# Retention and a gated convolution on one core: from one head's 128-row tile at a time to chunks of all heads with a running state, x kept on chip, and the convolution on TensorE

## The chip, the core and the metric

The kernel runs on one core of a Trainium2 chip. Its time is what the device measures from start to end, in microseconds. Each kernel is timed several times; of the kernel before three runs are given: 1052.33 us in the median, 1052.18 to 1053.14. The profile is of one execution, and its span (first to last instruction) was 1050.2 us.

## The reference

Inputs are q, k and v, each (batch 8, heads 8, positions 576, 64 columns) in float32, two weight matrices 512 x 512 and five rows of convolution weights 5 x 512.

```
scores = q @ k.T / 8                              # per batch and head
ret    = scores * gamma[h] ** (i - j) for i >= j, 0 otherwise
attn   = ret @ v                                  # gamma[h] = 1 - 2 ** (-5 - h)
x      = heads side by side: (batch, 576, 512)
gate   = sigmoid(sum over kk of conv_w[kk] * x shifted down by 4 - kk positions)
out    = (gate * (x @ w_val)) @ w_out             # (8, 576, 512) float32
```

## The kernel before

The work stands in two stages, and the order inside each is the order in which the program's loops write it.

The first stage loops over 8 batches and 8 heads. For one head it takes the 576 positions as four tiles of 128 and one of 64. Each tile of k and q is loaded (L86, 128 rows of 64 floats, one DMA on SyncE's queue, three buffers for all of them), cast to bfloat16 on GpSimd (L87), transposed on TensorE (L88) and copied from PSUM by ScalarE (L89). v is loaded and cast (L94, L95). Then, for each query tile, a loop over the key tiles up to it makes the scores (L103, contraction over 64 rows), multiplies them by a decay table on VectorE (L106 on the diagonal, L109 under it) and adds their product with v into one PSUM tile (L112). A head has 15 such blocks, the program 960. The result is cast on ScalarE (L115) and written to a tensor `xT` in device memory (L116), transposed: columns of the model by positions, in bfloat16.

The second stage loops over batches and, in each, over the position tiles. It loads a batch's `xT` (L146) with four zero columns in front. For each of four blocks of 128 columns it makes x @ w_val in four matmuls of 128 columns (L153), makes the convolution on VectorE in one multiplication (L157) and four multiply-adds (L159) over shifted slices, applies the sigmoid on ScalarE (L163) and multiplies gate and value on VectorE (L164). Four matmuls of 512 columns (L167) make the output tile, ScalarE copies it (L170) and SyncE's queue writes it out (L171). All DMAs of both stages are issued by SyncE.

The lines that the change replaces most are these of the innermost loops:

```
sc_ps = ps.tile([sk, sq], F32)
nc.tensor.matmul(sc_ps, lhsT=kall[:, j0:j0 + sk], rhs=qall[:, i0:i0 + sq], start=True, stop=True)
nc.vector.scalar_tensor_tensor(g, in0=xT_sb[:, dop, c0 + kk:c0 + kk + sz],
                               scalar=cw_sb[:, kk, dop:dop + 1], in1=g, op0=ALU.mult, op1=ALU.add)
```

Of the kernel before, what the change touches and what calls it, by code (L numbers as in the profile page):

```python
# [17 lines left out]


@with_exitstack  # L20
def kernel(
# [20 lines left out]
    dec_pool = ctx.enter_context(tc.tile_pool(name="dec", bufs=16))
    sb = ctx.enter_context(tc.tile_pool(name="sb", bufs=3))
    actx = ExitStack()
    vpool = actx.enter_context(tc.tile_pool(name="vp", bufs=2))
    ps = actx.enter_context(tc.tile_pool(name="ps", bufs=2, space=bass.MemoryType.PSUM))
    ops = actx.enter_context(tc.tile_pool(name="ops", bufs=2, space=bass.MemoryType.PSUM))

    q_tiles = [(i, min(128, S - i)) for i in range(0, S, 128)]
    j_tiles = q_tiles  # L50

    dec_full = {}
    dec_diag = {}
    gammas = {}
    for h in range(H):
        gamma = 1.0 - 2.0 ** (-5.0 - h)
        gammas[h] = gamma
        lng = math.log(gamma)
        it = sb.tile([128, 128], mybir.dt.int32)
        nc.gpsimd.iota(it, pattern=[[1, 128]], base=0, channel_multiplier=-1)  # L60
        ftf = sb.tile([128, 128], F32)
        nc.scalar.activation(ftf, it, AF.Exp, scale=lng)
        ftfull = dec_pool.tile([128, 128], BF16, tag=f"df{h}", bufs=1)
        nc.gpsimd.tensor_copy(ftfull, ftf)
        ftd = dec_pool.tile([128, 128], BF16, tag=f"dd{h}", bufs=1)
        nc.scalar.activation(ftd, ftf, AF.Copy, scale=scale)
        nc.gpsimd.affine_select(ftd, ftd, pattern=[[1, 128]], base=0,
                                channel_multiplier=-1, compare_op=ALU.is_ge, fill=0.0)
        dec_full[h] = ftfull
        dec_diag[h] = ftd  # L70

    from concourse.masks import make_identity
    ident = consts.tile([128, 128], BF16)
    make_identity(nc, ident)
    tps = actx.enter_context(tc.tile_pool(name="tps", bufs=2, space=bass.MemoryType.PSUM))

    for b in range(B):
        for h in range(H):
            kall = sb.tile([D, S], BF16)
            qall = sb.tile([D, S], BF16)  # L80
            for (j0, sk) in j_tiles:
                for src, dst in ((k, kall), (q, qall)):
                    tmpf = sb.tile([128, D], F32, tag="ttmpf")
                    tmp = sb.tile([128, D], BF16, tag="ttmp")
                    tp = tps.tile([D, 128], BF16)
                    nc.sync.dma_start(out=tmpf[:sk], in_=src[b, h, j0:j0 + sk, :])  # L86
                    nc.gpsimd.tensor_copy(tmp[:sk], tmpf[:sk])  # L87
                    nc.tensor.transpose(tp, tmp, ident)  # L88
                    nc.scalar.copy(dst[:, j0:j0 + sk], tp[:, :sk])  # L89
            v_tiles = {}  # L90
            for (j0, sk) in j_tiles:
                v_sbf = vpool.tile([sk, D], F32, tag=f"vsbf{j0}")
                v_sb = vpool.tile([sk, D], BF16, tag=f"vsb{j0}")
                nc.sync.dma_start(out=v_sbf, in_=v[b, h, j0:j0 + sk, :])  # L94
                nc.gpsimd.tensor_copy(v_sb, v_sbf)  # L95
                v_tiles[j0] = v_sb
# [105 lines left out]
```

## Time and profile before

| what | value |
| --- | --- |
| timed runs, median of 3 | 1052.33 us (1052.18 to 1053.14) |
| span of the profiled execution | 1050.2 us, 15367 instructions |
| TensorE matmuls (PE) | 680.8 us busy, 65%, 3360 of them |
| TensorE weight loads (PEld) | 349.4 us, 33% |
| VectorE (DVE) | 463.3 us, 44% |
| ScalarE (ACT) | 296.3 us, 28% |
| GpSimd (POOL) | 233.3 us, 22% |
| DMA | 164813 packets, 50.35 MB, of which 154992 packets under 512 B |

The profiled execution is the one that all rows come from; its span is its own time, and the timed runs stand 2.1 us above it. A busy share is an average over the whole span, so it is read stage by stage. The first stage ends at about 808 us. A matmul's busy time holds its way through the array, so that matmuls that follow each other overlap in it; how fast the array takes them is read from when they start.

### The profile page before, as it was taken

The page shows a single profiled execution, that of the slowest core. Times are in us where ns is not written, and L with a number is a line of the kernel's source. Part 1 is how long each engine was busy: PE and PEld are TensorE (multiplying, and loading weights), DVE is VectorE, ACT ScalarE, POOL GpSimd, SP SyncE. Part 2 cuts the span into 40 slices and gives each one's busy share as a digit, 9 for nine tenths or more (in the row PEclk, how much of TensorE's full clock was granted, in tenths as well). Part 3 has the DMA queues.
Part 4 walks back from the last instruction along what each step waited for, and adds up shares of the span by engine and source line. Part 5 has one row for each costly group of instructions (what it writes and reads, how often), then busy time and mean ns, then how long its engine had stood idle before and what let it go on. Part 6 is the DMA issues. An engine that isn't in the chain of part 4 may idle for free.

```text
span 1050.2 us, 15367 instructions
## 1 busy us (share of the span) xinstructions
PE 680.8 (65%) x3360; PEld 349.4 (33%) x3360; DVE 463.3 (44%) x1928; ACT 296.3 (28%) x1178; POOL 233.3 (22%) x992
## 2 busy tenths in 40 slices
PE   3676666666666666666666666666664567666665
PEld 1333333333333333333333333333332333333332
DVE  1332322222223322223322222222232999999998
ACT  3322222222222222222222222222222233232322
POOL 5222222222222222222222222222222000000000
PEclk9999999999999999999999999999999999998555
DMA  2111111121111111122111111112213121111211
GB/s 78 40 40 44 42 42 41 43 45 42 43 41 42 43 42 41 42 44 44 43 41 42 41 42 41 43 40 45 44 43 90 50 69 58 69 62 64 69 35 46
DMA packets 164813, 50.35 MB, mean 48 GB/s; under 512 B 154992, under 2 KB 159088, under 8 KB 164720
## 3 DMA queue, kind: packets, MB, share of 16 engines
q1 hardware_dynamic: 164720, 49.38, 19.3%
q14 instruction: 67, 0.55, 0.2%
q8 instruction: 26, 0.43, 0.2%
HBM read 35.14 MB, written 14.16 MB: 47 GB/s over the span
## 4 chain that ended last, share of the span: by engine, by line
PE 29%; DMA 28%; DVE 20%; issue 8%; ACT 8%; SPq 4%; POOL 3%; POOLq 1%; ACTq 0%; DVEq 0%
DMA tmpf<-in_q_dram 12%; DVE g L159 12%; PE o_ps L112 10%; PE sc_ps L103 10%; DMA tmpf<-in_k_dram 10%; PE tp L88 7%; DMA v_sbf<-in_v_dram 5%; ACT qall L89 5%; DVE zT L164 3%; POOL tmp L87 3%; DVE g L157 2%; ACT o_sb L115 2%; SPq L116 1%; PE op L167 1%; SPq L86 1%
## 5 line engine op out<-in xcount | busy, mean ns | idle before, releaser
L109 DVE SCALAR_TENSOR_TENSOR d_sb<-sc_ps,ftfull 128x128 bf16<-128x128 f32 (+1 forms) x640 | 151.4, 261 | 431.3 <-PE sc_ps L103 422.9
L112 PE MATMUL o_ps<-d_sb,v_sb 128*64 128x128 bf16 (+2 forms) x960 | 256.6, 268 | 52.5 <-DVE d_sb L109 18.5
L103 PE MATMUL sc_ps<-qall,kall 64*128 64x128 bf16 (+2 forms) x960 | 205.3, 266 | 114.8 <-ACT qall L89 114.1
L88 PE MATMUL tp<-ident,tmp 128*64 128x128 bf16 x640 | 187.3, 313 | 114.8 <-POOL tmp L87 101.5
L87 POOL CAST tmp<-tmpf 128x64 bf16<-128x64 f32 (+1 forms) x640 | 149.7, 236 | 494.3 <-DMA tmpf<-in_k_dram 217.9
L103 PEld LDWEIGHTS <-kall 64*128 64x128 bf16 (+1 forms) x960 | 97.8, 102 | 244.1 <-issue 191.1
L159 DVE SCALAR_TENSOR_TENSOR g<-xT_sb,cw_sb,g 128x128 f32<-128x128 bf16 (+1 forms) x640 | 175.8, 331 | 0.3
L88 PEld LDWEIGHTS <-tmp 128*64 128x64 bf16 x640 | 79.1, 132 | 218.1 <-POOL tmp L87 159.3
L106 DVE TENSOR_TENSOR d_sb<-sc_ps,ftd 128x128 bf16<-128x128 f32 (+1 forms) x320 | 87.8, 274 | 141.2 <-PE sc_ps L103 140.4
L112 PEld LDWEIGHTS <-v_sb 128*64 128x64 bf16 (+1 forms) x960 | 117.4, 136 | 72.0 <-POOL v_sb L95 10.1
L115 ACT CAST o_sb<-o_ps 64x128 bf16<-64x128 f32 (+1 forms) x320 | 79.4, 248 | 199.5 <-issue 120.8
L89 ACT COPY qall<-tp 64x128 bf16<-64x128 bf16 (+1 forms) x320 | 79.4, 248 | 199.3 <-PE tp L88 191.1
L89 ACT COPY kall<-tp 64x128 bf16<-64x128 bf16 (+1 forms) x320 | 79.6, 249 | 175.4 <-PE tp L88 173.5
L167 PE MATMUL op<-w_out_sb,zT 128*128 128x512 bf16 (+1 forms) x160 | 97.8, 620 | 35.4 <-DVE zT L164 35.3
L153 PE MATMUL vp<-xT_sb,w_val_sb 128*128 128x128 bf16 (+1 forms) x640 | 88.7, 293 | 48.1 <-DVE zT L164 40.1
L153 PEld LDWEIGHTS <-w_val_sb 128*128 128x128 bf16 x640 | 66.8, 137 | 95.2 <-issue 94.6
L95 POOL CAST v_sb<-v_sbf 128x64 bf16<-128x64 f32 (+1 forms) x320 | 75.4, 236 | 76.2 <-DMA v_sbf<-in_v_dram 67.1
L163 ACT ACTIVATE g<-g 128x128 f32<-128x128 f32 (+1 forms) x160 | 47.7, 299 | 134.8 <-DVE g L159 132.0
L157 DVE TENSOR_SCALAR g<-xT_sb,cw_sb 128x128 f32<-128x128 bf16 (+1 forms) x160 | 43.4, 272 | 7.8 <-DMA xT_sb<-xT 7.8
L164 DVE TENSOR_TENSOR zT<-g,vp 128x128 bf16<-128x128 f32 (+1 forms) x160 | 43.4, 272 | 1.4 <-ACT g L163 0.4
L167 PEld LDWEIGHTS <-zT 128*128 128x128 bf16 (+1 forms) x160 | 20.2, 127 | 67.1 <-DVE zT L164 65.6
L170 ACT COPY o_sb<-op 128x512 f32<-128x512 f32 (+1 forms) x40 | 23.4, 585 | 33.7 <-PE op L167 33.4
(16 smaller groups left out, 18.2 us busy)
## 6 DMA issues: line engine op xcount, KB each, us to landing
tmpf<-in_k_dram SPq DMA_DIRECT2D x256, 32.0 KB, 1.8
tmpf<-in_q_dram SPq DMA_DIRECT2D x256, 32.0 KB, 1.8
v_sbf<-in_v_dram SPq DMA_DIRECT2D x256, 32.0 KB, 1.8
out_dram<-o_sb SPq DMA_DIRECT2D x32, 256.0 KB, 2.0
xT_sb<-xT SPq DMA_DIRECT2D x8, 576.0 KB, 3.9
xT<-o_sb SPq DMA_DIRECT2D x256, 16.0 KB, 1.8
v_sbf<-in_v_dram SPq DMA_DIRECT2D x64, 16.0 KB, 1.9
w_val_f<-in_moe_w_val_dram SPq DMA_DIRECT2D x1, 1024.0 KB, 5.6
```

The source lines that it names most:

```text
L87: nc.gpsimd.tensor_copy(tmp[:sk], tmpf[:sk])
L88: nc.tensor.transpose(tp, tmp, ident)
L89: nc.scalar.copy(dst[:, j0:j0 + sk], tp[:, :sk])
L95: nc.gpsimd.tensor_copy(v_sb, v_sbf)
L103: nc.tensor.matmul(sc_ps, lhsT=kall[:, j0:j0 + sk], rhs=qall[:, i0:i0 + sq], start=True, stop=True)
L106: nc.vector.tensor_tensor(d_sb, sc_ps, dec_diag[h][:sk, :sq], op=ALU.mult)
L109: nc.vector.scalar_tensor_tensor(d_sb, in0=sc_ps, scalar=c, in1=dec_full[h][:sk, :sq], op0=ALU.mult, op1=ALU.mult)
L112: nc.tensor.matmul(o_ps, lhsT=v_sb, rhs=d_sb, start=(ji == 0), stop=(ji == len(jts) - 1))
L115: nc.scalar.copy(o_sb, o_ps)
L153: nc.tensor.matmul(vp, lhsT=w_val_sb[:, do, dop * P:(dop + 1) * P], rhs=xT_sb[:, do, pad + c0:pad + c0 + sz], start=(do == 0), stop=(do == ...
L159: nc.vector.scalar_tensor_tensor(g, in0=xT_sb[:, dop, c0 + kk:c0 + kk + sz], scalar=cw_sb[:, kk, dop:dop + 1], in1=g, op0=ALU.mult, op1=AL ...
L167: nc.tensor.matmul(op, lhsT=zT[:, dp, :sz], rhs=w_out_sb[:, dp, :], start=(dp == 0), stop=(dp == DOUT - 1))
```

## The change

The program is written anew, with the order of all instructions as the program states it.

- All eight heads are handled at once. A chunk is 128 positions of one batch (32 such chunks), or the last 64 positions of two batches (four tail chunks): 36 chunks. A chunk's k, q and v come in one DMA each into a 128 x 512 tile (two for a tail), 256 bytes to a packet since one head's row has 64 floats. Loads are issued six chunks ahead, weights on ScalarE's queue.
- The decay is split into a factor per key position, multiplied into v on GpSimd (`cast`), and one per query position, multiplied into the result on VectorE (`take_x`). The scores are only masked.
- Scores are made within a chunk alone. What earlier chunks give comes from a running sum of k times v per head (`update`, `take_state`, `carried`), kept in PSUM and copied to a block-diagonal bfloat16 tile.
- The result x stays in on-chip memory, bfloat16, columns by positions, four batches to a tile; nothing is written to device memory between the stages.
- The convolution is made on TensorE: per tap a 64 x 64 diagonal matrix, 40 matmuls of 256 columns for each unit. A unit is two chunks of the second stage.
- The loop runs over slots. In slot t come the loads of chunk t + 6, casts of t + 4, scores of t + 1, values of t, the state of t, transposes of t + 2; an even slot also has the convolution, gate and value product of unit t // 2 - 1, an odd one its output product.

The core of the diff (the tables of decay factors, masks, diagonals and weights are built once ahead of the loop and left out here):

```diff
--- before.py
+++ after.py
...
-    xT = dram.tile([B, DM, S], BF16)
...
-    for b in range(B):
-        for h in range(H):
...
+    half = ctx.enter_context(tc.tile_pool(name="half", bufs=2))
+    bfp = ctx.enter_context(tc.tile_pool(name="bfp", bufs=4))
+    tp_sb = ctx.enter_context(tc.tile_pool(name="tsb", bufs=3))
+    pp = ctx.enter_context(tc.tile_pool(name="pp", bufs=2))
+    gp = ctx.enter_context(tc.tile_pool(name="gp", bufs=2))
+    op_sb = ctx.enter_context(tc.tile_pool(name="osb", bufs=3))
+    xp = ctx.enter_context(tc.tile_pool(name="xp", bufs=1))
+    ps_t = ctx.enter_context(tc.tile_pool(name="pst", bufs=1, space=PSUM))
+    ps_s = ctx.enter_context(tc.tile_pool(name="pss", bufs=1, space=PSUM))
+    ps_o = ctx.enter_context(tc.tile_pool(name="pso", bufs=1, space=PSUM))
+    ps_st = ctx.enter_context(tc.tile_pool(name="psst", bufs=1, space=PSUM))
+    ps_g = ctx.enter_context(tc.tile_pool(name="psg", bufs=3, space=PSUM))
+    chunks = []
+    for g in range(B // GB):
+        for b in range(g * GB, (g + 1) * GB):
+            chunks += [("full", b, c) for c in range(NCH)]
+        chunks += [("tail", b, NCH) for b in range(g * GB, (g + 1) * GB, 2)]
+    NT = len(chunks)
...
+        def load_chunk(b, c):
+            for name, src in (("k", k), ("q", q), ("v", v)):
+                t = half.tile([P, H, D], F32, name=f"f{name}c", bufs=LA + 1)
+                nc.sync.dma_start(out=t, in_=src[b, :, c * P:(c + 1) * P, :].rearrange("h p d -> p h d"))
+                loaded[name, "full", b, c] = t
+        def load_tail(b):
+            for name, src in (("k", k), ("q", q), ("v", v)):
+                t = half.tile([P, H, D], F32, name=f"f{name}c", bufs=LA + 1)
+                for i in range(2):
+                    nc.sync.dma_start(out=t[i * TAIL:(i + 1) * TAIL],
+                                      in_=src[b + i, :, NCH * P:S, :].rearrange("h p d -> p h d"))
+                loaded[name, "tail", b, NCH] = t
...
+        load(0)
+        load(1)
+        cwn = consts.tile([KC * NP, P], F32, name="cwn")
+        nc.scalar.dma_start(out=cwn, in_=moe_conv_w.rearrange("k (o i) -> (k o) i", i=P))
+        wvf = consts.tile([P, NP, DM], F32, name="wvf")
+        wof = consts.tile([P, NP, DM], F32, name="wof")
+        nc.scalar.dma_start(out=wvf, in_=moe_w_val.rearrange("(o i) n -> i o n", i=P))
+        load(2)
+        wo_src = moe_w_out.rearrange("(pr ab hl p) n -> ab hl p pr n", pr=2, ab=2, hl=2)
+        for (p0, blk, ab, hl) in ((0, 0, 0, 0), (64, 0, 1, 0), (0, 2, 1, 1), (64, 2, 0, 1)):
+            nc.scalar.dma_start(out=wof[p0:p0 + 64, blk:blk + 2, :], in_=wo_src[ab, hl])
+        for t in range(3, LA - 2):
+            load(t)
...
+        def cast(t):
+            kind, b, c = chunks[t]
+            kb = bfp.tile([P, H, D], BF16, name="kb")
+            qb = bfp.tile([P, H, D], BF16, name="qb")
+            vb = bfp.tile([P, H, D], BF16, name="vb")
+            nc.gpsimd.tensor_copy(kb, loaded["k", kind, b, c])
+            nc.gpsimd.tensor_copy(qb, loaded["q", kind, b, c])
+            nc.gpsimd.tensor_tensor(vb, loaded["v", kind, b, c],
+                                    gin[:, c, :].unsqueeze(2).to_broadcast([P, H, D]), op=ALU.mult)
+            bf[t] = (kb, qb, vb)
+        tsb = {}
+        def turn(t):
+            kb, qb, vb = bf[t]
+            ps = ps_t.tile([P, 2, NP, P], BF16, name="tps")
+            for i, src in enumerate((kb, qb)):
+                flat = src.rearrange("p h d -> p (h d)")
+                for pr in range(NP):
+                    nc.tensor.transpose(ps[:, i, pr, :], flat[:, pr * P:(pr + 1) * P], ident)
+            kt = tp_sb.tile([P, NP, P], BF16, name="kt")
+            qt = tp_sb.tile([P, NP, P], BF16, name="qt")
+            nc.vector.tensor_copy(kt, ps[:, 0])
+            nc.scalar.copy(qt, ps[:, 1])
+            tsb[t] = (kt, qt)
+        def scores(t):
+            kt, qt = tsb[t]
+            s = [ps_s.tile([P, NP, P], F32, name=f"s{i}") for i in range(2)]
+            for pr in range(NP):
+                for i in range(2):
+                    r = slice(i * 64, i * 64 + 64)
+                    nc.tensor.matmul(s[i][:, pr, :], lhsT=kt[r, pr, :], rhs=qt[r, pr, :],
+                                     start=(pr == 0), stop=(pr == NP - 1), skip_group_check=True)
+            sps[t] = s
+        def masks(t, i):
+            m = mask if chunks[t][0] == "full" else mask_t
+            p = pp.tile([P, NP, P], BF16, name=f"p{i}")
+            nc.vector.tensor_tensor(p, sps[t][i], m.unsqueeze(1).to_broadcast([P, NP, P]), op=ALU.mult)
+            pt[t, i] = p
+        def carried(t):
+            kind, b, c = chunks[t]
+            o = ps_o.tile([P, NP, P], F32, name="o")
+            ops[t] = o
+            qt = tsb[t][1]
+            if kind == "full":
+                if c:
+                    for pr in range(NP):
+                        nc.tensor.matmul(o[:, pr, :], lhsT=state[b][:, pr, :], rhs=qt[:, pr, :],
+                                         start=(pr == 0), stop=False, skip_group_check=True)
+            else:
+                for pr in range(NP):
+                    for i in range(2):
+                        cs = slice(i * TAIL, (i + 1) * TAIL)
+                        nc.tensor.matmul(o[:, pr, cs], lhsT=state[b + i][:, pr, :], rhs=qt[:, pr, cs],
+                                         start=(pr == 0 and i == 0), stop=False, skip_group_check=True)
+        def values(t):
+            kind, b, c = chunks[t]
+            vb = bf[t][2]
+            o = ops[t]
+            fresh = kind == "full" and c == 0
+            for pr in range(NP):
+                for i in range(2):
+                    r = slice(i * 64, i * 64 + 64)
+                    nc.tensor.matmul(o[r, pr, :], lhsT=vb[:, 2 * pr + i, :], rhs=pt[t, i][:, pr, :],
+                                     start=(fresh and pr == 0), stop=(pr == NP - 1), skip_group_check=True)
+        def take_x(t):
+            kind, b, c = chunks[t]
+            x = xg[b // GB]
+            bl = b % GB
+            if kind == "full":
+                i0 = c * P
+                nc.vector.tensor_tensor(x[:, bl, :, PAD + i0:PAD + i0 + P], ops[t], gout[:, :, i0:i0 + P], op=ALU.mult)
+            else:
+                i0 = NCH * P
+                for i in range(2):
+                    nc.vector.tensor_tensor(x[:, bl + i, :, PAD + i0:PAD + S],
+                                            ops[t][:, :, i * TAIL:(i + 1) * TAIL], gout[:, :, i0:S], op=ALU.mult)
+        def update(t):
+            kind, b, c = chunks[t]
+            if kind != "full":
+                return
+            kb, qb, vb = bf[t]
+            if c == 0:
+                st[b] = ps_st.tile([P, NP, P], F32, name="st")
+            kf, vf = (s.rearrange("p h d -> p (h d)") for s in (kb, vb))
+            for pr in range(NP):
+                cs = slice(pr * P, (pr + 1) * P)
+                nc.tensor.matmul(st[b][:, pr, :], lhsT=kf[:, cs], rhs=vf[:, cs],
+                                 start=(c == 0 and pr == 0), stop=(c == NCH - 1 and pr == NP - 1),
+                                 skip_group_check=True)
+        def take_state(t):
+            kind, b, c = chunks[t]
+            if kind != "full":
+                return
+            s = sbl[b % GB] if c == NCH - 1 else sbd[c % 2]
+            for i in range(2):
+                r = slice(i * 64, i * 64 + 64)
+                nc.scalar.copy(s[r, :, i * 64:i * 64 + 64], st[b][r, :, i * 64:i * 64 + 64])
+            state[b] = s
+        def xs(n, rows, blk, shift):
+            kind, b, c = chunks[2 * n]
+            x = xg[b // GB]
+            if kind == "full":
+                c0 = c * P + shift
+                return x[rows, b % GB, blk, c0:c0 + 2 * P]
+            c0 = NCH * P + shift
+            return x[rows, :, blk, c0:c0 + TAIL]
+        def conv(n):
+            g = [ps_g.tile([P, 2, 2 * P], F32, name="g") for _ in range(2)]
+            lo, hi = slice(0, 64), slice(64, 128)
+            for pr in range(2):
+                a, b = 2 * pr, 2 * pr + 1
+                for kk in range(KC):
+                    for (rows, blk, cols, bank) in ((lo, a, lo, 0), (hi, b, lo, 1), (lo, b, hi, 0), (hi, a, hi, 1)):
+                        nc.tensor.matmul(g[bank][cols, pr, :], lhsT=dg[rows, blk, kk, :], rhs=xs(n, rows, blk, kk),
+                                         start=(pr == 0 and kk == 0), stop=(pr == 1 and kk == KC - 1),
+                                         skip_group_check=True)
+            gps[n] = g
+            gsb[n] = []
+        def gate(n, i):
+            t = gp.tile([P, 2, 2 * P], F32, name=f"gate{i}")
+            nc.scalar.activation(t, gps[n][i], AF.Sigmoid)
+            gsb[n].append(t)
+        def value(n, i):
+            vps = ps_g.tile([P, 2, 2 * P], F32, name="g")
+            for j in range(2):
+                for o in range(NP):
+                    nc.tensor.matmul(vps[:, j, :], lhsT=wvb[:, o, 2 * i + j, :], rhs=xs(n, slice(0, P), o, PAD),
+                                     start=(j == 0 and o == 0), stop=(j == 1 and o == NP - 1), skip_group_check=True)
+            z = gp.tile([P, 2, 2 * P], BF16, name=f"z{i}")
+            nc.vector.tensor_tensor(z, gsb[n][i], vps, op=ALU.mult)
+            zsb[n, i] = z
+        def project(n, i):
+            kind, b, c = chunks[2 * n]
+            o = ps_g.tile([P, DM], F32, name="g")
+            for j in range(NP):
+                nc.tensor.matmul(o, lhsT=zsb[n, j // 2][:, j % 2, i * P:(i + 1) * P], rhs=wob[:, j, :],
+                                 start=(j == 0), stop=(j == NP - 1))
+            ob = op_sb.tile([P, DM], F32, name="ob")
+            nc.scalar.copy(ob, o)
+            if kind == "full":
+                c0 = (c + i) * P
+                nc.sync.dma_start(out=out[b, c0:c0 + P, :], in_=ob)
+            else:
+                for j in range(2):
+                    nc.sync.dma_start(out=out[b + 2 * i + j, NCH * P:S, :], in_=ob[j * TAIL:(j + 1) * TAIL])
+        ok = lambda t: 0 <= t < NT
+        cast(0)
+        cast(1)
+        for slot in range(-2, NT + 2):
+            t = slot
+            n = t // 2 - 1
+            unit = 0 <= n < NT // 2
+            odd = t % 2 == 1
+            if t >= 0 and ok(t + LA - 2):
+                load(t + LA - 2)
+            if ok(t + 4):
+                cast(t + 4)
+            if ok(t + 1):
+                scores(t + 1)
+                masks(t + 1, 0)
+            if ok(t):
+                values(t)
+                take_x(t)
+            if ok(t + 1):
+                masks(t + 1, 1)
+            if unit and not odd:
+                conv(n)
+            if ok(t):
+                update(t)
+                take_state(t)
+            if ok(t + 2):
+                turn(t + 2)
+            if t == -2:
+                prep_conv()
+            if t == -1:
+                prep_wv()
+            if t == 0:
+                prep_wo()
+            if unit and not odd:
+                gate(n, 0)
+                gate(n, 1)
+                value(n, 0)
+                value(n, 1)
+            if unit and odd:
+                project(n, 0)
+                project(n, 1)
+            if ok(t + 1):
+                carried(t + 1)
```

## Rows read from the trace of the kernel before

**Rows 1.** The page's 40 equal slices, busy tenths of two engines.

```profile
PE   3676666666666666666666666666664567666665
...
DVE  1332322222223322223322222222232999999998
```

**Rows 2.** The chain that ended last: shares of the span, by engine and line.

```profile
PE 29%; DMA 28%; DVE 20%; issue 8%; ACT 8%; SPq 4%; POOL 3%; POOLq 1%; ACTq 0%; DVEq 0%
DMA tmpf<-in_q_dram 12%; DVE g L159 12%; PE o_ps L112 10%; PE sc_ps L103 10%; DMA tmpf<-in_k_dram 10%; PE tp L88 7%; DMA v_sbf<-in_v_dram 5%; ACT qall L89 5%; DVE zT L164 3%; POOL tmp L87 3%; DVE g L157 2%; ACT o_sb L115 2%; SPq L116 1%; PE op L167 1%; SPq L86 1%
```

**Rows 3.** Windows: PE, PEld, DVE, ACT, POOL busy (count); clock, DMA share, GB/s.

```profile
20.00:780.00 760.00, 502.81 (x2456) 260.71 (x2455) 224.41 (x922) 210.16 (x919) 212.53 (x913) 1.00 0.19 42
...
890.00:960.00 70.00, 48.56 (x246) 23.55 (x246) 69.51 (x299) 21.23 (x61) 0.00 (x0) 1.00 0.17 59
960.50:963.80 3.30, 1.34 (x12) 0.60 (x10) 3.30 (x15) 0.88 (x3) 0.00 (x0) 1.00 0.60 195
964.00:1050.00 86.00, 56.19 (x282) 27.28 (x282) 80.80 (x342) 25.65 (x73) 0.00 (x0) 0.50 0.14 49
```

**Rows 4.** Costliest groups: line, operation, count, busy, mean ns, idle before.

```profile
L159 DVE SCALAR_TENSOR_TENSOR g<-xT_sb,cw_sb,g 128x128 f32<-128x128 bf16 (+1 forms) x640 | 175.8, 331 | 0.3
...
L157 DVE TENSOR_SCALAR g<-xT_sb,cw_sb 128x128 f32<-128x128 bf16 (+1 forms) x160 | 43.4, 272 | 7.8 <-DMA xT_sb<-xT 7.8
```

**Rows 5.** PE timeline: start us, merged time us, line, tiles, count.

```profile
958.88 0.61 PE L153 MATMUL vp<-xT_sb,w_val_sb 128*128 128x128 bf16 x4
...
961.54 0.38 PE L153 MATMUL vp<-xT_sb,w_val_sb 128*128 128x128 bf16 x4 [0.90 <-DVE zT L164]
961.76 0.38 PE L167 MATMUL op<-w_out_sb,zT 128*128 128x512 bf16 x1
...
964.97 0.63 PE L153 MATMUL vp<-xT_sb,w_val_sb 128*128 128x128 bf16 x4
```

**Rows 6.** DMA issues: tile, queue, count, KB each, median us to landing.

```profile
tmpf<-in_k_dram SPq DMA_DIRECT2D x256, 32.0 KB, 1.8
...
out_dram<-o_sb SPq DMA_DIRECT2D x32, 256.0 KB, 2.0
xT_sb<-xT SPq DMA_DIRECT2D x8, 576.0 KB, 3.9
...
out_dram<-o_sb SPq DMA_DIRECT2D x8, 128.0 KB, 2.4
```

**Rows 7.** Groups by shape: busy us, mean ns, idle before.

```profile
L87 POOL CAST tmp<-tmpf 128x64 bf16<-128x64 f32 x512 | 120.6, 237 | 430.3 <-DMA tmpf<-in_k_dram 207.1 <-DMA tmpf<-in_q_dram 132.7 <-PE sc_ps L103 51.3
...
L153 PE MATMUL vp<-xT_sb,w_val_sb 128*128 128x128 bf16 x512 | 76.2, 306 | 42.0 <-DVE zT L164 34.0 <-DMA xT_sb<-xT 8.0
...
L115 ACT CAST o_sb<-o_ps 64x128 bf16<-64x128 f32 x256 | 66.3, 259 | 72.4 <-PE o_ps L112 66.3 <-PE tp L88 0.7
...
L163 ACT ACTIVATE g<-g 128x128 f32<-128x128 f32 x128 | 39.5, 309 | 117.5 <-DVE g L159 114.8
L164 DVE TENSOR_TENSOR zT<-g,vp 128x128 bf16<-128x128 f32 x128 | 36.5, 286 | 0.2 <-PE vp L153 0.2
...
L170 ACT COPY o_sb<-op 128x512 f32<-128x512 f32 x32 | 18.8, 586 | 26.7 <-PE op L167 26.6
...
L115 ACT CAST o_sb<-o_ps 64x64 bf16<-64x64 f32 x64 | 13.2, 206 | 127.1 <-issue 120.8 <-PE o_ps L112 6.3
...
L163 ACT ACTIVATE g<-g 128x64 f32<-128x64 f32 x32 | 8.2, 257 | 17.3 <-DVE g L159 17.3
...
L164 DVE TENSOR_TENSOR zT<-g,vp 128x64 bf16<-128x64 f32 x32 | 7.0, 218 | 1.2 <-ACT g L163 0.4
...
L125 POOL CAST w_val_sb<-w_val_f 128x2048 bf16<-128x2048 f32 x1 | 1.9, 1887 | 0.0
```

**Rows 8.** SP's DMA issues at the start: start us, time us.

```profile
0.80 0.39 SPq L86 DMA_DIRECT2D tmpf<-in_k_dram  x1
1.24 0.41 SPq L86 DMA_DIRECT2D tmpf<-in_q_dram  x1
```

More of the change, by code (lines that the diff above doesn't have):

```diff
@@ L17 @@
 ALU = mybir.AluOpType
+PSUM = bass.MemoryType.PSUM
 @with_exitstack
@@ L34 @@
     DM = moe_w_val.shape[0]
-    assert D == 64 and DM == H * D
+    KC = moe_conv_w.shape[0]
+    P = 128
+    NP = H // 2
+    NCH = S // P
+    TAIL = S - NCH * P
+    PAD = KC - 1
+    GB = 4
+    LA = 8
+    assert D == 64 and DM == H * D and TAIL == 64 and B % GB == 0 and NP == 4
     scale = 1.0 / math.sqrt(D)
-    dram = ctx.enter_context(tc.tile_pool(name="dram", bufs=1, space=bass.MemoryType.DRAM))
-    xT = dram.tile([B, DM, S], BF16)
+    lng = [math.log(1.0 - 2.0 ** (-5.0 - h)) for h in range(H)]
@@ L41 @@
     consts = ctx.enter_context(tc.tile_pool(name="c", bufs=1))
[L42 to L54, printed above, removed]
-    for h in range(H):
[L56 to L75, printed above, removed]
-    for b in range(B):
-        for h in range(H):
[L79 to L96, printed above, removed]
-            for (i0, sq) in q_tiles:
-                o_ps = ops.tile([D, sq], F32)
-                jts = [jt for jt in j_tiles if jt[0] <= i0]
-                for ji, (j0, sk) in enumerate(jts):
-                    v_sb = v_tiles[j0]
-                    sc_ps = ps.tile([sk, sq], F32)
-                    nc.tensor.matmul(sc_ps, lhsT=kall[:, j0:j0 + sk], rhs=qall[:, i0:i0 + sq], start=True, stop=True)
-                    d_sb = sb.tile([sk, sq], BF16)
-                    if j0 == i0:
-                        nc.vector.tensor_tensor(d_sb, sc_ps, dec_diag[h][:sk, :sq], op=ALU.mult)
-                    else:
-                        c = scale * (gammas[h] ** (i0 - j0))
-                        nc.vector.scalar_tensor_tensor(d_sb, in0=sc_ps, scalar=c,
-                                                       in1=dec_full[h][:sk, :sq],
-                                                       op0=ALU.mult, op1=ALU.mult)
-                    nc.tensor.matmul(o_ps, lhsT=v_sb, rhs=d_sb,
-                                     start=(ji == 0), stop=(ji == len(jts) - 1))
-                o_sb = sb.tile([D, sq], BF16)
-                nc.scalar.copy(o_sb, o_ps)
-                nc.sync.dma_start(out=xT[b, h * D:(h + 1) * D, i0:i0 + sq], in_=o_sb)
@@ L130 @@
-    cw_sb = consts.tile([P, Kc, DOUT], F32)
-    with nc.allow_non_contiguous_dma(reason="conv"):
-        for kk in range(Kc):
-            nc.sync.dma_start(out=cw_sb[:, kk, :], in_=moe_conv_w[kk].rearrange("(do di) -> di do", di=P))
-    xp = ctx.enter_context(tc.tile_pool(name="xp", bufs=2))
-    zp = ctx.enter_context(tc.tile_pool(name="zp", bufs=2))
-    vps = ctx.enter_context(tc.tile_pool(name="vps", bufs=2, space=bass.MemoryType.PSUM))
-    opo = ctx.enter_context(tc.tile_pool(name="opo", bufs=2, space=bass.MemoryType.PSUM))
```

119 lines of the change are left out of this document (75 added, 44 removed).

## The prediction

> **What bounds the kernel now.** I read the page's slices first, then the chain that ended last, then each stage by its windows. The slices [rows 1] show two stages. In the first 31 slices PE stands at 6 or 7 tenths and DVE at 2 or 3; behind them DVE is at 9. The chain [rows 2] says what the first stage lacks: its largest pieces are landings of single loads (k 10%, q 12%, v 5%), then PE, ACT and POOL steps of one head that follow each other. That is latency, one 128-row tile of one head at a time, for 64 heads. The second stage is DVE: in 890 to 960 us it is busy 69.5 of 70 us [rows 3], nearly all of it the five tap products (640 of 331 ns and 160 of 272 ns, 219 us together [rows 4]).
>
> Two more things are to be seen, because they set the floor of the changed kernel.
> TensorE's clock. The windows grant 1.00 before 960.5 us and 0.50 after 964 [rows 3]. But four 128-column matmuls take 0.61 us before 960.5, 0.63 after 964, and 0.38 only in between [rows 5]. So the 1.00 ahead of 960.5 doesn't describe the array: by its own spacing it runs at the level of 1.2 GHz there too, and at 2.4 GHz in those 3.3 us alone. At the upper level the next group starts 0.22 us after four such matmuls (961.54 to 961.76): 55 ns for 128 columns with their weight load hidden. At the lower level it is (0.63 less 0.31 for one of them [rows 7]) / 3 = 107 ns.
> The DMA engines. In 20 to 780 us, where nearly every packet has 256 B, they moved 42 GB/s at a share of 0.19 [rows 3], so 42 / 0.19 = 221 GB/s if they were never idle. In 890 to 960 (1152 and 2048 B) it is 59 / 0.17 = 347 GB/s.
>
> **The change, part by part.** All of it goes together: heads side by side in one 128 x 512 tile, 36 chunks of 128 tokens instead of 960 score blocks, the lower blocks replaced by a running 64 x 64 state, taps on TensorE, x kept in SBUF. The old 1050.2 us fall away whole, so the new time is a sum of its own: start, 17 pairs of slots, end. A pair of slots handles two chunks and one unit (two chunks' worth) of the second stage.
>
> DMA per pair. The loads are 28.3 MB, again as 256 B runs (one head's 64 floats), 110,592 of them as before, but 1024 in an instruction instead of 128. 28.3 / 221 = 128 us, 3.56 us a chunk. The output is 9.44 MB in 2048 B rows: 27 us, 1.51 a unit. The weights are 2.1 MB: 6 us. The xT round trip (4.7 MB each way) is gone. A pair costs 2 x 3.56 + 1.51 = 8.6 us. No row shows a 1024-packet load. Bounds: a 512-packet load of 576 KB lands in 3.9 us [rows 6], 131 packets per us counting its latency, which would make 110592 / 131 = 844 us; below, the 347 GB/s of long packets would make 28.3 / 0.347 = 82 us. I take 128 us, since that is the busy time of this very packet size.
>
> TensorE per pair, in steps of 128 columns: transposes 16, scores 16, carried state 8, values 16, state update 8, taps 40 x 2 = 80, value projection 16 x 2 = 32, output projection 8 x 4 = 32; together 208. At 55 ns that is 11.4 us if each matmul has the array to itself. Scores come in pairs on the two row halves, values on the two column halves, taps on all four quarters. If those run side by side, 8 + 8 + 60 steps fall away: 132 x 55 = 7.3 us. Every K = 64 matmul of before uses the same row half, so no row decides it. I take 7.3, because the operands share neither rows, columns nor bank, and keep 11.4.
> On this the Trainium skill speaks both ways (TensorEngine Tiling, Key Properties): tiles "operate independently", but changing the tiling mode drains the engine; Restrictions and Gotchas adds that column tiling disables fast weight load. By the first rule a pair is 7.3, by its absence 11.4, and the drains come on top; no run here shows it.
> Between shapes of different row and column counts I add 0.1 us per change, about one cold 128-column step, seven times a pair: 0.7 us (from 0 to 1.4).
>
> DVE per pair: 4 masks, 2 kt copies, 2 x products, 2 gate products, all of 512 columns. From 286 ns at 128 and 218 at 64 columns [rows 7], 1.06 ns a column: 693 ns, so 6.9 us. ACT: qt 2 and output 2 of 586 ns (a row), two sigmoids of 309 + 384 x 0.81 = 620, four state copies of 259 + 128 x 0.83 = 365: 5.1 us. POOL: a cast of 512 by 237 at 64 and 1887 at 2048 columns is 610 ns, four of them; the v product with two inputs isn't shown, between 0.6 (a cast) and 1.2 (two passes); I take 1.2: 4.8 us. These three lie beside PE and DMA.
>
> Waits that the order adds. In an even slot PE meets value(n,1), whose PSUM bank is the first tap bank, free only after gate(n,0). ACT reaches that after the state copies (from 1.85 us of the slot on, 0.73), qt (0.59) and the gate (0.62): 3.8 us. PE is there at 3.2, so it loses 0.6; behind it stand z1, carried and the next scores. On SP, load(t+6) stands behind the output DMAs, which wait for ACT's copy; six chunks of lead cover that, and without it a load would be late by one slot. POOL's cast(t+4) waits for update(t), with two slots to spare. The 80 steps of taps move from DVE to PE; x no longer waits for a transfer (3.9 us each, eight times).
>
> So PE needs 7.3 + 0.6 + 0.7 = 8.6 us a pair, exactly what DMA needs. Two chains of one length that wait for each other lose something; I allow 0.3 (an estimate, half the gate's wait): 8.9.
>
> Sum. Slot 1 turns chunk 3, so it needs four chunks and the weights, which share the engines: 4 x 3.56 + 6 + 2.6 (0.8 to the first issue as before, 1.8 landing [rows 6]) = 22.8, and 1 us for casts and turn: slot 2 starts at 24. That hides POOL's constants and ACT's tables. Then 17 x 8.9 = 151. At the end slots 36 and 37 have no retention: taps 1.1, gate and value 2.5, projection 1.8, copy 0.6, the output landing 2.4 [rows 6]: 8.4. Span 183; the timed median stood 2.1 above the span, so 185 us.
>
> **Rivals.** An order and layout that don't work as drawn give these.
> - No side-by-side matmuls. PE 11.4 + 1.3 = 12.7 a pair: 24 + 216 + 11 + 2 = 253 us. For it: nothing of the kind ran before. Against: disjoint rows, columns and banks. With taps two at a time it is 24 + 17 x 10 + 11 + 2 = 207, within my range.
> - TensorE stays at 1.2 GHz. 132 x 107 = 14.1, with the switches 14.8 a pair: 24 + 252 + 13 + 2 = 291 us. For it: in the second stage PE sat at that level almost throughout, at 48.6 busy of 70 us [rows 3]. Against: those were DVE's waits; here the array would be the bound and never wait at that level. The Trainium skill (TensorE: Matmul & The Clock Gate, Part 1) says that activity releases the throttle, which speaks against this rival, while its Part 4 says that transposes don't count as busy in the same way; here they are 16 of 132 steps.
> - Loads slower when saturated. If the packets come no faster than the start's issue of a 128-packet load each 0.45 us [rows 8], 284 packets per us, 110592 / 284 = 389 us and 35 for start, end and output: 424 us. For it: no stretch shows more. Against: there the issue was the limit, and the packets kept the engines a fifth busy.
> - Slower than before. If one load's 1024 packets go at the pace of a 128-packet load from issue to landing, 1.8 us [rows 6], 71 per us, the loads take 1555 us. It decides from 110592 / 1015 = 109 packets per us down. Against: the 512-packet load already reaches 131 with its latency counted.
>
> **How the numbers follow.** Forecast 185 us, chance 0.66, own range 160 (each pair at 7.6, better overlap, and a start of 20) to 212 (pair at 10.3). No side-by-side 0.13; low clock 0.07; slow loads 0.06; slower than before 0.01; below 160, if packets overlap better than their busy time says, 0.07. The range 158 to 256 takes in the first two; what lies outside is about 0.2. A difference of 0.2% (2 us) is what a measurement of this kernel can tell: faster 0.985, same 0.005, slower 0.01.
>
> **What would show it.** DMA share near 0.9 with PE gaps released by casts: the load term right. Four taps starting within about 110 ns at clock 1.00: side by side; four in 430 ns: not. Rows of PE at 0.50 in mid-kernel: the clock rival. PE waiting for a gate by ACT once a pair, about 0.6 us: the PSUM term. DVE over 80% of the span: I have mis-sized its 512-column pass. A first full pair well before or after 24 us: the start. The prediction is wrong if neither PE nor DMA fills the middle of the span.

## The result and the profile after

The changed kernel takes 195.45 us (194.65 to 196.56, 4 runs), 0.186 of the time before (0.185 to 0.1865). The forecast was 185 us. The profiled execution has a span of 194.1 us. Executions over 1.5% longer than the shortest of the same kernel are left out of every median and ratio below; the profiles of e1, e4 and e8 are of such executions.

First its page: busy us with share and count per engine, the 40 slices, the DMA queues, and the chain that ended last.

```profile
PE 152.2 (78%) x2273; PEld 111.0 (57%) x2273; DVE 114.3 (59%) x211; ACT 89.3 (46%) x183; POOL 86.9 (45%) x126
...
PE   0112666998898989898988899788989898979990
...
DVE  6406774747475657575766657474766575747420
...
DMA  5999999999999999799999795999997998931124
...
q1 hardware_dynamic: 117760, 37.76, 86.3%
q10 hardware_dynamic: 1134, 2.11, 4.2%
...
PE 48%; DMA 18%; ACT 12%; DVE 9%; SPq 4%; issue 4%; POOL 1%; ACTq 0%; DVEq 0%; POOLq 0%
```

Where PE stood at 6 tenths for three quarters of the time and the DMA engines at a share of 0.19 [rows 1, 3], PE now stands at 8 to 9 tenths and the DMA engines at 9 as well. The windows (columns as in [rows 3]) say it more sharply: from 24 to 140 us the DMA share is about 1 and PE is busy for eight to nine tenths. The granted clock is 1.00, the level of 2.4 GHz, but for one stretch, the level of 1.2 GHz from 35.1 to 38.5 us, shown last.

```profile
0.00:24.00 24.00, 5.83 (x53) 3.94 (x53) 11.79 (x33) 8.22 (x14) 10.93 (x27) 1.00 0.97 202
24.00:60.00 36.00, 30.27 (x468) 22.35 (x468) 22.72 (x39) 17.49 (x36) 21.77 (x28) 0.95 1.11 227
60.00:100.00 40.00, 35.89 (x562) 26.99 (x552) 25.24 (x46) 20.28 (x43) 18.80 (x26) 1.00 0.98 230
100.00:140.00 40.00, 35.37 (x536) 25.68 (x532) 25.94 (x46) 18.67 (x41) 19.89 (x27) 1.00 0.99 224
...
175.00:195.00 20.00, 13.83 (x186) 8.88 (x182) 7.13 (x14) 6.81 (x13) 0.00 (x0) 0.93 0.26 79
...
35.10:38.50 3.40, 3.40 (x36) 2.62 (x34) 2.64 (x5) 0.73 (x2) 1.91 (x4) 0.50 1.30 227
```

One pair of slots on PE's timeline (start, merged time, line, count, idle before). From scores to scores it is 112.48 - 103.40 = 9.08 us, and this repeats: the taps (L322) of 15 consecutive pairs start 9.15 us apart on the mean, 12 of them within 8.9 and 9.1.

```profile
103.40 0.40 PE L220 MATMUL s<-qt,kt 64*128 64x128 bf16 x8 [0.53 <-ACT qt L209]
103.73 0.41 PE L261 MATMUL o<-p,vb 128*64 128x128 bf16 x8
104.08 1.31 PE L322 MATMUL g<-xg,dg 64*64 64x256 bf16 x40
105.31 0.40 PE L289 MATMUL st<-vb,kb 128*128 128x128 bf16 x4
105.55 0.39 PE L205 MATMUL tps<-ident,kb 128*128 128x128 bf16 x4
105.77 0.39 PE L205 MATMUL tps<-ident,qb 128*128 128x128 bf16 x4
105.99 1.04 PE L337 MATMUL g<-xg,wvb 128*128 128x256 bf16 x8
107.79 1.04 PE L337 MATMUL g<-xg,wvb 128*128 128x256 bf16 x8 [0.75 <-ACT gate L330]
108.67 0.39 PE L244 MATMUL o<-qt,sbd 128*128 128x128 bf16 x4
...
110.34 1.89 PE L347 MATMUL g<-wob,z 128*128 128x512 bf16 x8
112.07 0.39 PE L244 MATMUL o<-qt,sbd 128*128 128x128 bf16 x4
112.48 0.40 PE L220 MATMUL s<-qt,kt 64*128 64x128 bf16 x8
```

Two waits stand in it: 0.75 us for the gate, and 0.53 for qt. The first returns in each of the middle pairs; the second is at its largest here, in the others of the middle it is 0.25 in every second pair and next to nothing between. ScalarE's order in that slot explains the first (same columns):

```profile
105.75 0.76 ACT L300 CAST sbd<-st 64x256 bf16<-64x256 f32 x2 [0.55 <-PE st L289]
106.65 0.59 ACT L209 COPY qt<-tps 128x512 bf16<-128x512 bf16 x1
107.14 1.09 ACT L330 ACTIVATE gate<-g 128x512 f32<-128x512 f32 x2
```

The taps were done at about 105.4 while ScalarE stood idle; the gates come behind the state copies and qt. The second wait comes through VectorE: it makes kt behind both masks, and qt, which reads the same PSUM tile, comes only after kt.

**Two bounds of one length.** By PE and its waits a pair is 9.08 us. By the DMA engines it is the same: q1's packets fill 0.863 x 194.1 = 167.5 us of them, the weights another 8.2, and of those 167.5 the trace's packet times put 138.5 on the 110,592 packets of 256 B (20.0 ns each) and 27.4 on the output. Loads and output of a pair are 138.5 / 18 + 27.4 / 18 = 9.2 us. A window's share of packet times can come out above 1 (1.11 above), so 9.2 is an estimate and no floor. From one execution it can't be read which of the two sets the pace. The runs below were made for that.

### The profile page after: what moved, and what is told of

Its sections match the earlier page's. It is cut to its first block, busy times and chain, and to the rows that moved or that the text cites. A ratio compares the mean times of both kernels' runs of the same rounds, so it can differ in the third digit from the quotient of the medians.

```text
span 194.1 us, 5639 instructions
## 1 busy us (share of the span) xinstructions
PE 152.2 (78%) x2273; PEld 111.0 (57%) x2273; DVE 114.3 (59%) x211; ACT 89.3 (46%) x183; POOL 86.9 (45%) x126
## 4 chain that ended last, share of the span: by engine, by line
PE 48%; DMA 18%; ACT 12%; DVE 9%; SPq 4%; issue 4%; POOL 1%; ACTq 0%; DVEq 0%; POOLq 0%
PE g L337 10%; PE g L347 9%; PE g L322 9%; DMA fvc<-in_v_dram 7%; ACT qt L209 6%; DMA out_dram<-ob 5%; DMA fkc<-in_k_dram 5%; PE tps L205 5%; PE s L220 5%; PE o L261 4%; ACT gate L330 4%; PE st L289 4%; DVE kt L208 4%; DVE p L229 3%; SPq L77 2%
## 5 line engine op out<-in xcount | busy, mean ns | idle before, releaser
L229 DVE TENSOR_TENSOR p<-s,mask 128x512 bf16<-128x512 f32 x64 | 43.7, 684 | 19.3 <-PE s L220 19.3
L337 PE MATMUL g<-xg,wvb 128*128 128x256 bf16 x288 | 37.1, 272 | 14.7 <-ACT gate L330 13.4
L193 POOL TENSOR_TENSOR vb<-fvc,gin 128x512 bf16<-128x512 f32 x36 | 37.5, 1043 | 22.2 <-DMA fvc<-in_v_dram 16.0
L340 DVE TENSOR_TENSOR z<-gate,g 128x512 bf16<-128x512 f32 x36 | 24.8, 688 | 33.4 <-ACT gate L330 24.7
L337 PEld LDWEIGHTS <-wvb 128*128 128x128 bf16 x288 | 27.3, 97 | 21.1 <-issue 18.3
L191 POOL CAST kb<-fkc 128x512 bf16<-128x512 f32 x36 | 22.9, 636 | 31.9 <-DMA fkc<-in_k_dram 21.1
L192 POOL CAST qb<-fqc 128x512 bf16<-128x512 f32 x36 | 22.2, 617 | 29.4 <-DMA fqc<-in_q_dram 29.2
L347 PE MATMUL g<-wob,z 128*128 128x512 bf16 x144 | 34.4, 380 | 0.3 <-DVE z L340 0.3
L322 PE MATMUL g<-xg,dg 64*64 64x256 bf16 x720 | 23.2, 271 | 0.0
L270 DVE TENSOR_TENSOR xg<-o,gout 128x512 bf16<-128x512 f32 x32 | 21.8, 681 | 0.0
L322 PEld LDWEIGHTS <-dg 64*64 64x64 bf16 x720 | 18.4, 106 | 2.0 <-issue 0.4
L261 PE MATMUL o<-p,vb 128*64 128x128 bf16 x288 | 15.4, 230 | 0.0
## 6 DMA issues: line engine op xcount, KB each, us to landing
wof<-in_moe_w_out_dram ACTq DMA_DIRECT2D x4, 256.0 KB, 10.5
```

The costliest lines, as they stand in the source:

```text
L191: nc.gpsimd.tensor_copy(kb, loaded["k", kind, b, c])
L193: nc.gpsimd.tensor_tensor(vb, loaded["v", kind, b, c], gin[:, c, :].unsqueeze(2).to_broadcast([P, H, D]), op=ALU.mult)
L229: nc.vector.tensor_tensor(p, sps[t][i], m.unsqueeze(1).to_broadcast([P, NP, P]), op=ALU.mult)
L261: nc.tensor.matmul(o[r, pr, :], lhsT=vb[:, 2 * pr + i, :], rhs=pt[t, i][:, pr, :], start=(fresh and pr == 0), stop=(pr == NP - 1), skip_gr ...
L322: nc.tensor.matmul(g[bank][cols, pr, :], lhsT=dg[rows, blk, kk, :], rhs=xs(n, rows, blk, kk), start=(pr == 0 and kk == 0), stop=(pr == 1 a ...
L337: nc.tensor.matmul(vps[:, j, :], lhsT=wvb[:, o, 2 * i + j, :], rhs=xs(n, slice(0, P), o, PAD), start=(j == 0 and o == 0), stop=(j == 1 and ...
```

## The experiments

Theory "chain": PE's order and its two waits set the pair, and the transfers only keep up. Theory "DMA": the packets do, and a wait that is saved comes back elsewhere. Each was timed beside the kernel before, on the same chip; the pairs are means over the starts of the taps of 15 pairs, the first and the last left out.

| run | us (median) | ratio to before, 95% | mean pair | first taps at |
| --- | --- | --- | --- | --- |
| the change | 195.45 | 0.185 to 0.1865 | 9.15 | 29.2 |
| e1 gate first | 193.93 | 0.1836 to 0.1853 | 9.35 | 30.2 |
| e2 no load of q | 194.70 | 0.1833 to 0.1853 | 9.04 | 28.1 |
| e3 gate first, kt first | 195.18 | 0.1841 to 0.186 | 9.27 | 28.6 |
| e4 e3 and no load of q | 174.30 | 0.1646 to 0.1662 | 7.92 | 31.3 |
| e5 e3, 8 output buffers | 187.37 | 0.1762 to 0.178 | 8.66 | 30.6 |
| e6 taps in turn | 232.02 (1 run) | | 11.1 | 28.9 |
| e7 e5, late weights | 186.95 | 0.1767 to 0.178 | 8.83 | 23.8 |
| e8 e3, runs of 512 B | 179.70 | 0.1692 to 0.172 | 7.92 | 34.9 |
| e9 e8, late weights, 8 buffers | 170.66 | 0.1612 to 0.1628 | 7.92 | 24.4 |
| e10 late weights alone | 193.86 | 0.1834 to 0.1841 | 9.06 | 24.3 |

**e1, the gates first.**

```diff
                 conv(n)
+                gate(n, 0)
+                gate(n, 1)
...
             if unit and not odd:
-                gate(n, 0)
-                gate(n, 1)
                 value(n, 0)
```

> ScalarE's two sigmoids of a unit are issued right behind the taps, ahead of the state copies and of qt. Theory chain (the pair of slots is set by TensorE and what it waits for, the DMA engines only keep up): the 0.75 us wait of the second value product for the gate goes, 17 pairs x 0.75 = 12.8 us, so about 183. Theory DMA (the loads' and stores' packets fill the engines, 176 us of them): within 2 us of 195, the saved wait comes back elsewhere on a load.

It took 193.93 us, and its interval touches the change's. In its profile the wait for the gate is gone, and three of the five pairs in which PE doesn't stand behind a store take 8.13 us instead of 9.05: the gate was worth 0.92 a pair. The other ten lose it again to waits for stores. Taken alone this speaks for DMA.

**e2, a third of the loads away.**

```diff
-            for name, src in (("k", k), ("q", q), ("v", v)):
+            for name, src in (("k", k), ("v", v)):
...
-            nc.gpsimd.tensor_copy(qb, loaded["q", kind, b, c])
+            nc.gpsimd.tensor_copy(qb, loaded["k", kind, b, c])
```

> q isn't loaded; the cast of q reads k's tile. Everything else is done as before, so the DMA engines have 46 us less to carry. Theory DMA: the middle is set by TensorE's chain instead and the start needs 2.4 us less a chunk: 195 falls to about 165 to 175. Theory chain: only the start is shorter, by at most 7 us: 188 or more.

194.70 us, the same again (q is left out, so this is a timing only), and the pair stays at 9.04 with the engines a fifth idle (window of e2, 60 to 140 us):

```profile
60.00:140.00 80.00, 71.47 (x1102) 53.23 (x1101) 51.65 (x91) 38.91 (x85) 39.00 (x54) 1.00 0.78 179
```

Taken alone this speaks for the chain, and 9.05 us is also what 12 of the change's 15 pairs take: there the chain sets the pace, and only the other three (9.33 to 9.98), in which ScalarE waits 1.8 to 2.5 us for a store, are longer. Neither theory in its pure form survives both runs: the transfers are the next limit, close behind.

**e3, both waits of PE away.** e1, and in odd slots:

```diff
-            if ok(t + 1):
+            if ok(t + 1) and not odd:
                 masks(t + 1, 1)
...
             if ok(t + 2):
                 turn(t + 2)
+            if ok(t + 1) and odd:
+                masks(t + 1, 1)
```

> The gates first as in e1_gate_first, and in odd slots the second mask behind the transposes and the copy of kt, so that qt and the next scores come 0.5 us earlier. Theory chain: 17 x (0.75 + 0.5) = 21 us less, about 174, if the DMA engines let it. Theory DMA: within 2 us of 195.

195.18 us. The pairs now differ: most take 7.8 to 8.1 us, the chain's own length, and every second or third takes 9 to 12. What ends the long ones is a new wait, first among e3's waits (total us, times, longest):

```profile
ACT ob L350 <- DMA out_dram<-ob: 35.4, 14, 4.7
DVE z L340 <- PE g L337: 27.7, 28, 3.9
```

In the change's own trace the first of them is smaller, and it has the gate's wait as well:

```profile
ACT ob L350 <- DMA out_dram<-ob: 14.1, 11, 2.5
PE g L337 <- ACT gate L330: 13.4, 16, 2.2
```

ScalarE waits for one of three output buffers whose store stands in SyncE's queue with the loads. The time saved at the gate is handed to the transfers, and one thing comes on top. In four of e3's long pairs TensorE waits 2.0 to 2.4 us, and the granted clock then falls to 0.50, the level of 1.2 GHz, for 3.4 us. One of the four (columns as in [rows 3]):

```profile
77.20:80.60 3.40, 3.34 (x16) 2.31 (x16) 0.69 (x1) 2.19 (x6) 1.22 (x2) 0.50 0.83 187
```

These four pairs take 11.2 to 12.2 us, where the one with a wait of 2.55 and no fall takes 10.7. So in this execution a part of what keeps e3 at the change's time is the clock.

**e4, both limits loosened.** e3 and e2 together.

> Both orders and no load of q: neither bound of today is left at its size. TensorE's pair without the two waits is 7.8 us: 17 x 7.8 + 22 start + 10 end = 165. If it comes well under both e2_no_q and e3_both_orders, chain and DMA are two bounds of nearly one length.

174.30 us. That is 9 above the 165 expected: the pairs are as foreseen, but the first taps came at 31.3 us, where 22 had been set for the start. Each edit alone is worth less than 1 us, both together 21: two bounds of nearly one length, as the mean pairs show (9.05 by the chain, about 9.2 by the packets, 7.9 with both loosened).

**e5, more output buffers.**

```diff
-    op_sb = ctx.enter_context(tc.tile_pool(name="osb", bufs=3))
+    op_sb = ctx.enter_context(tc.tile_pool(name="osb", bufs=8))
```

> Both orders of e3 and eight output buffers instead of three, so that ScalarE needn't wait for an output to land behind queued loads (35 us of waits in e3). If those waits are only where the DMA limit shows, the pair stays at the DMA engines' 9.2 us on the average and the time at 190 to 195. If the buffers themselves were the limit, pairs of 8.0 us follow and the time is 176 to 180.

187.37 us, below the first range and above the second: I had no case for a mixture. Its first six pairs take 7.8 to 8.3 us and the later ones 8.3 to 9.7. The two stretches of e5 show PE giving way while the DMA share stays full:

```profile
30.00:90.00 60.00, 59.24 (x935) 44.72 (x940) 42.73 (x74) 33.87 (x73) 31.24 (x42) 1.00 1.01 227
90.00:160.00 70.00, 63.21 (x940) 45.71 (x950) 45.34 (x78) 35.09 (x75) 35.53 (x47) 1.00 1.06 236
```

The chain runs ahead as long as the early loads last, and the stores may fall behind by eight buffers; then the packets set the pace. PE waits for casts there (tps for qb, 12.7 us in 14 waits), where the change has such waits only at its start. Its granted clock stays at 1.00 from 33.9 to 184 us, so a part of its gain over e3 may be that e3's falls are gone; no run separates the two. This version computes the reference's output and beats both kernels.

**e6, the taps of one quarter behind each other.**

```diff
-            for pr in range(2):
-                a, b = 2 * pr, 2 * pr + 1
-                for kk in range(KC):
-                    for (rows, blk, cols, bank) in ((lo, a, lo, 0), (hi, b, lo, 1), (lo, b, hi, 0), (hi, a, hi, 1)):
+            for q4 in range(4):
+                for pr in range(2):
+                    a, b = 2 * pr, 2 * pr + 1
+                    rows, blk, cols, bank = ((lo, a, lo, 0), (hi, b, lo, 1), (lo, b, hi, 0), (hi, a, hi, 1))[q4]
+                    for kk in range(KC):
```

> The changed kernel with the taps of one array quarter behind each other instead of the four quarters in turn; same 40 matmuls, same sums. If the four quarters do run side by side (1.3 us a unit), it needs 40 x 110 ns = 4.4 us, 3.1 more in each of 18 units: 195 + 53 = about 248, somewhat less if the gate's wait hides in it. If side by side isn't what makes it 1.3 us, the time stays.

232.02 us: the pair grows from 9.1 to 11.1. One unit's taps, of e6:

```profile
121.19 3.39 PE L323 MATMUL g<-xg,dg 64*64 64x256 bf16 x40
```

3.39 us instead of 1.31. 2.08 us more in each of 18 units is 37 us, the whole difference. It isn't the 4.4 expected: inside a quarter the starts are about 110 ns apart, as one 256-column matmul alone needs, but at a change of quarter the next one's taps began while the last one's still ran, in part two at a time. In the change each of four taps starts within 8 ns of the one before it, and the next four follow 100 to 104 ns later (unit at 104 us). So the quarters do run side by side, and it is the turn-taking order of the taps that uses it.

**e7 and e10, the weights behind the first chunks.** e7 is e5 with this, e10 is the change with this alone:

```diff
-        nc.scalar.dma_start(out=wvf, in_=moe_w_val.rearrange("(o i) n -> i o n", i=P))
         load(2)
+        nc.sync.dma_start(out=wvf, in_=moe_w_val.rearrange("(o i) n -> i o n", i=P))
+        load(3)
...
-            nc.scalar.dma_start(out=wof[p0:p0 + 64, blk:blk + 2, :], in_=wo_src[ab, hl])
+            nc.sync.dma_start(out=wof[p0:p0 + 64, blk:blk + 2, :], in_=wo_src[ab, hl])
...
-            if t == -1:
+            if t == 1:
                 prep_wv()
-            if t == 0:
+            if t == 2:
                 prep_wo()
```

> e5 with the two weight matrices loaded by SyncE's queue behind the third and fourth chunk, and prepared in slots 1 and 2, so that ScalarE doesn't stand 9 us in the issue of its four DMAs before it makes the decay factors. Theory: slot 2 starts about 5 us earlier than 28 us, limited by four chunks of loads; if DMA sets the middle, the end moves by less, 1 to 4 us against e5.

> The changed kernel with the late weights alone. The first taps come at 24 instead of 29 us; the pairs are at 9.05 by the chain and 9.2 by the DMA engines. If the engines' total sets the end, 193 to 196 as before; if the chain does, 190 to 191.

In both the first taps come 5 to 7 us earlier, and the end moves little: 186.95 against 187.37, their intervals overlapping and less than the 1 to 4 us expected, and 193.86 against 195.45 for e10. In e7 the second unit's taps are 4.2 us ahead of e5's and the last unit's 1.7: the pairs between have 2.5 us more of waits for casts. e10's time lies in the range for DMA, but for another reason: its middle pairs lie within 0.25 us of the chain's 9.05, and what was gained is lost in the first, where the second unit's taps start at 41.3 us, as in the change (40.9). These are rows of PE in that pair of e10:

```profile
24.30 2.35 PE L323 MATMUL g<-xg,dg 64*64 64x256 bf16 x40
...
28.11 0.61 PE L206 MATMUL tps<-ident,kb 128*128 128x128 bf16 x4 [0.92 <-POOL kb L192]
30.11 0.61 PE L206 MATMUL tps<-ident,qb 128*128 128x128 bf16 x4 [1.40 <-POOL qb L193]
30.52 1.91 PE L338 MATMUL g<-xg,wvb 128*128 128x256 bf16 x8
33.76 1.87 PE L338 MATMUL g<-xg,wvb 128*128 128x256 bf16 x8 [1.33 <-ACT gate L331]
```

Two waits are for casts behind loads, 2.3 us. But the taps take 2.35 us instead of 1.31 and a value product 1.9 instead of 1.04: by its own spacing TensorE runs at the level of 1.2 GHz here until 39.2 us, although the column of the granted clock says 1.00. In the change four 128-column matmuls take 0.61 us at 24.2 us and 0.40 from 25.8 on, and its first pair has the low level only for the 3.4 us shown above, behind a wait of 2.17 for the first gate. e2, with a third of the loads away, has the second unit's taps at 41.4 as well, with no wait of PE for a load in between, and with rows at the low level up to 31.8 us and from 35.2 to 38.6. So the loads alone don't take e10's gain back; the clock takes part of it, and no run sets the share of each.

**e8 and e9, half as many packets for the same bytes.** Output positions and heads stand elsewhere in both, so they are timings only.

```diff
-                nc.sync.dma_start(out=t, in_=src[b, :, c * P:(c + 1) * P, :].rearrange("h p d -> p h d"))
+                h0, s0 = 4 * (c % 2), 256 * (c // 2)
+                nc.sync.dma_start(out=t.rearrange("p (h two) d -> p h (two d)", two=2),
+                                  in_=src[b, h0:h0 + 4, s0:s0 + 256, :].rearrange("h (p two) d -> p h (two d)", two=2))
```

> Both orders of e3; each load of a full chunk takes the same bytes in half as many runs of 512 B (four heads, two positions to a partition, so the output is not the reference's: positions and heads stand elsewhere). If the count of packets is what fills the DMA engines, the loads' 138 us fall to about 95 and the chain of 8.0 us a pair sets the time: 174 to 178, as in e4. If the bytes do, it stays at 193 to 196.

> e8 (both orders, runs of 512 B, so the output is not the reference's) with the late weights of e7 and eight output buffers. In e8 ScalarE stood 16.4 us in its issue of the weights and the first taps came at 34.9 us. Theory: the start then was that stand; with it gone the first taps come at about 24 us, the pairs stay at 8.0, and 181 falls by 8 to 11, to 170 to 173. If the start was only the loads' arrival, it stays at 178 to 181.

e8 took 179.70 us, above its range by 2; its first taps came late (34.9 us), and its pairs are at 7.92, as foreseen. Its load packets fill 94.4 us at 512 B (30.7 ns each) and 13.8 at 256 B (the tails) instead of 138.5. e9 puts the start right as well: first taps at 24.4, 170.66 us, in its range. In 60 to 140 us of e9 PE is busy without a gap:

```profile
60.00:140.00 80.00, 79.47 (x1268) 60.35 (x1275) 58.81 (x104) 45.98 (x99) 44.43 (x62) 1.00 0.93 257
```

The bytes are those of the change. So it is the count of short packets, more than the bytes, that fills the engines there. The Trainium skill (DMA: Bandwidth & Descriptors, Specifications) asks for transfers of 512 B or more for line rate; the direction agrees, but here 512 B in 30.7 ns is 16.7 B per ns and engine, against 12.8 at 256 B and 21.5 for the output's 2048 B in 95 ns.

## Why the prediction was right, and by how much each term was off

The sum was 24 + 151 + 8.4 + 2.1 = 185.5, given as 185. Measured on PE: slot 2 begins at 28.55 us, slot 36 at 183.64, the span ends at 194.13, and the median stands 1.32 above it: 28.55 + 155.09 + 10.49 + 1.32 = 195.45.

- **The bound.** "Exactly what DMA needs": that PE's chain and DMA would be of nearly one length was right, and it is what e1 to e4 show. I forecast 8.6 for each; it was 9.05 and about 9.2. The 0.3 allowed for two chains that wait for each other was 0.1 (9.15 against 9.05); that the pair still came out near 8.9 is in part luck, as a larger gate's wait filled the allowance.
- **Loads, 128 us.** 138.5. The packet of 256 B took 20.0 ns, where 42 GB/s at a share of 0.19 [rows 3] stands for 18.5. The trace has 27 ns in the second ten microseconds, with the weights beside the loads, 18 to 22.5 later. Output 27 forecast, 27.4 measured; weights 6 and 8.2.
- **Side by side, 7.3 us.** Right. Taps in 1.31 us where 1.1 was forecast, scores eight in 0.40. Two of the four taps at a time do write one bank, other than I wrote, and it did no harm. PE's pair without waits, changes of shape included, is 7.9 (e4, e9), against 8.0 forecast. The Trainium skill (TensorEngine Tiling, Key Properties) has tiles that operate independently; the runs agree, e6 most plainly.
- **The gate's wait, 0.6 us.** 0.75 of idle time, and 0.92 a pair when it is taken away (e1), in the place and by the order that was named. The wait for qt I missed; it is 0.25 in every second pair.
- **The start, 24 us.** 28.55, and for another reason than loads. I wrote that the loads would hide "POOL's constants and ACT's tables". ScalarE's queue at the start of the change shows what stands ahead of its tables:

```profile
1.48 0.41 ACTq L102 DMA_DIRECT2D wvf<-in_moe_w_val_dram  x1
1.92 9.00 ACTq L106 DMA_DIRECT2D wof<-in_moe_w_out_dram  x4
10.96 1.28 ACT L139 ACT_TABLE_LOAD   x1 [10.96 <-DMA fqc<-in_q_dram]
12.25 0.24 ACT L139 ACTIVATE gin<-gin 128x40 f32<-128x40 f32 x1
12.39 3.12 ACT L147 ACTIVATE gout<-posi,lsc,lcol 128x576 f32<-128x576 int32 x4
15.43 0.56 ACT L209 COPY qt<-tps 128x512 bf16<-128x512 bf16 x1
```

  Four issues of weight loads hold the engine for 9 us, and the first qt comes at 15.4. The weights also delay chunk 0's q, whose cast starts at 10.35 us, in e10 at 6.00. e8 tells the two apart: there that cast starts at 7.15, and the first qt still comes at 20.92, behind 14.5 us of issues. With the weights later and on SyncE's queue the first taps come at 24 (e7, e9, e10): the 24 us would have been right for that kernel. In e10 the gain is lost again in the first pair.
- **The end, 8.4 us.** 10.5 from the last taps. The last unit's taps and value products take 3.2 us, its projection ends 5.5 us in, and copies and the last stores follow one another.
- **VectorE and the others.** 684 ns for the mask product against 693, 1043 for POOL's v product against 1200, 601 for the gate against 620: none of them over 60% of the span, as was said. kt took 421, not 693: this bfloat16 copy out of PSUM was quicker than the products with float32 (684).
- **The first and the last pair.** That 17 pairs together were off by only 4 us is in part luck. By the starts of the taps the first took 11.6 us (the wait of 2.17 for the first gate, whose table is loaded there, and 3.4 us at the low clock) and the last 5.5 (no transposes left, no wait); the sum had neither.
- **Clock.** 1.00 from 38.5 to 192 us, with 55 ns for 128 columns (value product: eight of 256 in 1.04 us). For the middle the rival of 1.2 GHz fell, as did slow loads and the slower kernel. At the start, up to 25 us and from 35.1 to 38.5, PE did run at that level, which the sum left out.

Of the 10.4 us by which the forecast was short, 4.1 are the pairs, 4.6 the start, 2.1 the end and 0.5 the rounding; 0.8 goes the other way, the time around the span.

## What to carry to other kernels

Where two bounds come out within a few per cent, each edit that loosens one of them alone measures as nothing; loosen both before giving either up. Work out transfers by packets as well as by bytes. Count what an engine issues ahead of its own work: the issues of four loads held ScalarE for 9 us here. And read TensorE's level from its rows: a wait costs more than its length when the level falls behind it.
